# Exponent matmuls over all 128 rows in place of pairs in 64 rows, with a re-made issue list

## The chip, the cores and the metric

The kernel runs on one core of one Trainium2 chip. The metric is the device time of one execution in microseconds (us); the median of three runs is given, with the lowest and highest.

## The reference

Two independent branches work on 2048 positions and 576 channels each, and their outputs stand side by side. Branch A is a diagonal state-space model used as a long convolution: a kernel K is made for every channel from 128 complex exponentials, and u is convolved with it. Branch B is linear attention of 32 heads of 18 with a learned feature map.

```python
# A
A = -exp(log_A_real) + 1j * A_imag
C = (C_real + 1j * C_imag) * dt[:, None]
P = exp((A * dt[:, None])[:, :, None] * pos)          # 576 x 128 x 2048
K = 2 * einsum("dn,dnl->dl", C, P).real
y = irfft(rfft(u_t, 2 * L) * rfft(K, 2 * L))[:, :, :L] + u * D_skip
# B
q, k, v = split(x @ wqkv)
phi = lambda t: concat([softmax(t @ w_phi), softmax(-(t @ w_phi))])
kv, z = einsum("bhsf,bhsd->bhfd", phi(k), v), phi(k).sum(s)
out = (einsum("bhqf,bhfd->bhqd", phi(q), kv) / (phi(q) . z + 1e-6)) @ wo
```

## The kernel before

The kernel first records some 2459 operations, each with the engine that may do it, what it reads and writes, and a cost that a planner used. It then issues them in the order of a long written list, `ORDER`. A word of the list is the number of an operation; an `x` takes its second engine (ACT or DVE, DVE or POOL), `@` names the PSUM banks that it gets, and `:n` puts n filler matmuls ahead of it, which multiply zeros (line 237). So the order on every engine, the banks and the choice of engine all come from this list. All transfers are issued from SyncE's queue, SP, in list order.

Branch B runs through 16 key tiles (projections as `x` times `wh`, `wl`, `vh`, `vl`, each number split in two parts, 14 matmuls of 288 columns per half), a small turn of the sums (`kv`), and 16 query tiles (projection, softmax, transposes of `e` into `fT`, products with `kvb`, output projection). Branch A has u transformed in 16 steps (`ub` times `w1`), 36 groups of 16 channels that make K, its transform (`kfirst`), 16 frequency products (`ub`, `ff`), and 16 closing steps (`last`, `zi` times `w1`). Both branches are interleaved by the list.

A group makes its part of K from cosines and sines (`cs`, by POOL and ACT) and from magnitudes exp(m t). The exponents m t come from TensorE: `mg` holds log magnitudes in four parts of 16 channels, that is 64 rows, and holds the same 64 rows a second time in rows 64 to 127; `sel` is a constant with the times. `sizes_of` (its matmuls have line 295 in the profile, as all of `mm` do) makes the exponents for two groups at once: six matmuls of 512 columns into six PSUM banks, `M`, `up` and `dn` for each group. They are three operations of two matmuls each; one works in rows 0 to 63 and the other in rows 64 to 127 of the array. Over the two halves `sel` holds different columns (at, dn, up above, up, at, dn below), so that a pair reads the same 512 columns of `sel` and yields two different results. There are 18 such calls, 54 pairs, 108 matmuls. ACT then takes exp in PSUM (line 811), DVE multiplies them into the waves (lines 815 to 820), and 64 small matmuls (`g4`) sum over the 128 states.

The tensor engine works in differently split arrays: the projections use all 128 rows and columns, the pairs and the u steps two halves of 64 rows, `g4` and the key sums four strips of 32 columns, the frequency products 64 x 32 and 32 x 64. `mode` in the recorded operation names this split for the planner.

A tile name such as `ub`, `ff`, `zi` or `ot` is a pool of 5, 2, 2 and 3 buffers in turn; a load into one waits for whoever read the buffer last.

Of the kernel before, what the change touches and what calls it, by code (L numbers as in the profile page):

```python
# [276 lines left out]
def body(tc, nc, i, out, ctx):  # L277
# [16 lines left out]
    def mm(o, l, r, start=True, stop=True, skip=False):  # L294
        pe.matmul(o, l, r, start=start, stop=stop, skip_group_check=skip)  # L295
# [492 lines left out]
    def sizes_of(g, par):  # L788
        pl.at("group", g // 2)
        pl.step("g0")  # L790
        mg, gi = par[1], g % (NG // NB)
        b = [B("ps", [128, W, 32]) for _ in range(6)]

        def both(k):
            def f():
                for r, rs in enumerate((lo, hi)):
                    mm(b[2 * k + r].t.rearrange("p x y -> p (x y)"), mg.t[rs, gi + (2 * k + r) // 3, :], sel.t[rs, 512 * k:512 * k + 512])
            op("pe", 233, f, r=[mg, sel], w=b[2 * k:2 * k + 2], mode=(64, 128))
        for k in range(3):
            both(k)  # L800
        return b[:3], b[3:]
# [191 lines left out]
0 1 2 3 1097 1093 4 68 1094 5 1096 1154 1104 1105 1107 1092 1108 1109 51 34 1095 6 27 7@0:49 20 1106 1110 1111 1112 1113 1114 1115 8 35@2 1199 1137 11  # L993
28@4 29 52 12 1116 1120 9 53x 30 36 10 54 13 22@6 32 37 21 1117 39 992 1118 1119 40 15@0 14 1074 23 31 33 1121 38 1063 1003 344 18 25 16 345 24
1004@42:11 19 26 17 41 1073 287 1127 1077 56@6 47 42 288 1078 48 1122 1124 346x 1123 57 347x 1125 43 1126 44 45 60 1396 1076 1084 1006 1128 1129 289x
1130 1080 61 49 1075 348@0 1400 46 1131 349 1079 290 1138 291@6 1132 1161 1133 1134 352 62 1081 292 295 353 296 1082 354 1085 351@2 1083 350 355x 1397
1048 294@0 59@6 1086 1399 1135 55 1136 63 268 269 1155 361 1005 64 58 356 69 71 270x 297 360 1162 1156 1157 1398 271x 65 1158 171 1087 1064@24 1066 72
1200 1163 293 273@6 272 357 66 67 73x 1159 1164 1160 1065 1088 298x 1089 50@4 299 358 1090 1168 74 1165 70 304 359 1166 1167 77@2 300 276 1139 1401
301 277 1402 362 172 173x 1169 1170 1192 302 76 274@0 1140 275 80 278 1141 1403 1091 1148 1147 279 1149 1150 174 303 1193 1201 1151@56 1172 111 1098
1171 81 82 1152@72 305 285x 1099 79@0 1180 1174 112 1173 1175 78 1177 1176 1153@35 89 1178@6 1067 1068 1194 1183 284 1202 1203 1181 1184 83 1204 1195  # L1000
113 114 84 1196 1018 1007 75 1038 1205 1230 1197 1198 211 1182 1179 280 1185 1186 281 1231 282 179@0 177@2 1142 176 116@6 117 325 115 175 1206 85 180
181 182 1207 1208 183x 86 1143 283x 286 1190@52 1232 1233 1234 120 121 87x 1187@3 1218 1189@67 1235 1237 1238 1239 326 122 1221 1188 178 327 1209 1404
212 189 1211 328x 123x 88 118@2 330@0 90 119 213x 124 1210 1212 1214 1213 1191@67 184 129 1215 185 1220 188 1240 1144 1241 1216@5 214 1242 216@2 215
1145 1146 1269 91 1243 128 1236 1223 186 306 1268 187x 1224 1219 1222 92 1217 93 1405 1270 1271 331@6 219 220 94 332 1100 329 221 222 125 190 126 1419
1245 1406 333 1225@5 342x 1276 1275 1272 1277 1227@23 1244 1278 1246 1228@67 1247 334 127x 1249 1256 1226x 1248 191 335 223 218@0 1250 1252 1251 1253
217 1279 192 1280 193 130 1254@5 1273 307 228 1274 1259 336 194 1307 1049@20 1306 224 225 1051 1050x 341 1308 96@6 1282 1229@01 1258 337 1281 1257 97
1407 1262 338 197@2 339 100 101 196 1261 1260 199@6 308x 1052 1283 1284 198 226x 195 1412 227 1408 1409 1410 1411 1413 1255 200 1414 229 201 340x 1101
1263@5 230 202 1440 1415 1265@10 1102 209 1069@62 102 343 1314 1070x 95 1058 203 1285 1071 1266@23 1288 1287 1290 1286 98@6 1291 99 309 1313 1309 1315
1294 1264 1267@15 1289 231 204 103 1297 1072 1295 205 109 1292@0 1293 1316 1317 1318 232 1298 1310 1311 233 1312 311@2 1417 104 1320 1296 1319 1321x
105 1039@60 1300 206 208 1041 1040 106 310 313@0 312 207x 1299 314 315 1416 1418 1420 1421 1422 1423 1424 1425 1491 1059@62 108 1322 316 1426 1427  # L1010
1428 1492 1103 1061 210 323x 317 1060 1301@5 1304@23 1042 1303@67 1323 1484 322 1493 993 1033 235@0 131 249 234 1325 1324 1485 1486 1326 1327 132 1328
237@6 1302 1329 238 239 250 251x 1330@5 1487 107x 1447 110 1488 1331x 252 1062 1305@25 1349 1351 1350 240 1332 236 1352 1446 1448 1353 1355 247 318
# [82 lines left out]
```

## Time and profile before

| | |
|---|---|
| median of three runs | 544.55 us (543.78 to 545.48) |
| profiled execution | 545.11 us |
| its span, first to last instruction | 543.3 us |
| PE busy | 521.5 us (96%), 8192 matmuls |
| DVE, ACT, POOL busy | 455.9, 382.1, 328.8 us |
| bytes moved by DMA | 107.01 MB, 197 GB/s on average |
| granted TensorE clock | 0.998 |

A row of a group has line, engine, operation, names (written <- read), shape, count, then busy time and mean length of one, then idle time of the engine just before and what ended it. Matmul records overlap, so the step between matmuls is read from their starts in the timeline. PEld is TensorE's weight load, SPq the issuing of transfers.

### The profile page before, as it was taken

Reading aid. Unit: us, or ns where it says so; the run is one execution under the profiler, and the core shown is the slowest. Engines: PE = TensorE matmul, PEld = TensorE weight load, DVE = VectorE, ACT = ScalarE, POOL = GpSimd, SP = SyncE. Lnnn points to the kernel's source line nnn. Section 1 sums busy time; section 2 is a strip of 40 time slices with the busy share of each in tenths; the row PEclk is TensorE's granted clock in tenths of the full one; section 3 lists DMA queues with packets and bytes.
Section 4 is the critical chain, followed back from the end, with each engine's and each line's share of the span. In section 5 each row is a group of like instructions: output and inputs, shape, how many; then the busy total and the mean of one; then the engine's idle time right before and its main releaser. Section 6 shows DMA issues by size and latency. Waiting matters only on the chain.

```text
span 543.3 us, 19242 instructions
## 1 busy us (share of the span) xinstructions
PE 521.5 (96%) x8192; PEld 435.9 (80%) x8192; DVE 455.9 (84%) x716; ACT 382.1 (70%) x555; POOL 328.8 (61%) x456
## 2 busy tenths in 40 slices
PE   8999999999999989999999999999899999999995
PEld 7999899888888767888878666766689877776984
DVE  7999899898868889999989996999974889787641
ACT  4868798798559799889689977989733444343332
POOL 1173885958777775982758998997433617434300
PEclk9999999999999999999999999999999999999999
DMA  8936711244245678246664588756458789998785
GB/s 235 326 105 195 281 45 31 101 139 134 89 139 190 207 241 294 83 128 196 229 205 118 153 265 250 241 180 194 131 173 271 234 281 293 287 281 260 265 252 157
DMA packets 86163, 107.01 MB, mean 197 GB/s; under 512 B 5698, under 2 KB 70338, under 8 KB 86078
## 3 DMA queue, kind: packets, MB, share of 16 engines
q1 hardware_dynamic: 86078, 105.79, 61.5%
q8 instruction: 64, 1.05, 0.8%
q14 instruction: 21, 0.17, 0.1%
HBM read 61.22 MB, written 44.54 MB: 195 GB/s over the span
## 4 chain that ended last, share of the span: by engine, by line
PE 69%; DVE 13%; DMA 7%; ACT 4%; issue 3%; SPq 2%; POOL 1%; DVEq 0%; ACTq 0%; POOLq 0%
PE psum L295 63%; PE psum L549 3%; DMA ff<-in_ff_dram 2%; DMA dram<-zi 2%; PE psum L237 2%; DVE ac L314 1%; DVE cs L816 1%; SPq L979 1%; PE psum L577 1%; DMA cs<-dram 1%; DVE e L310 1%; DMA ub<-dram 1%; DVE e L314 1%; DVE small L434 1%; DVE small L437 1%
## 5 line engine op out<-in xcount | busy, mean ns | idle before, releaser
L295 PE MATMUL psum<-vh,x 128*128 128x288 f32 x576 | 123.6, 301 | 0.5 <-ACT ks L300 0.5
L295 PE MATMUL psum<-wh,x 128*128 128x288 f32 x576 | 124.1, 302 | 0.0
L757 POOL TENSOR_TENSOR cs<-cs,pi 128x32 int32<-128x32 int32 (+4 forms) x180 | 108.5, 608 | 8.0
L295 PEld LDWEIGHTS psum<-wh,x 128*128 128x128 f32 x576 | 94.1, 188 | 7.7 <-issue 4.2
L295 PEld LDWEIGHTS psum<-vh,x 128*128 128x128 f32 x576 | 94.0, 188 | 5.4 <-issue 3.2
L295 PE MATMUL psum<-vl,x 128*128 128x288 f32 x320 | 93.8, 295 | 0.0
L295 PE MATMUL psum<-wl,x 128*128 128x288 f32 x320 | 93.7, 295 | 0.0
L811 ACT ACTIVATE psum<-psum 128x512 f32<-128x512 f32 x108 | 59.9, 588 | 15.4 <-PE psum L295 14.9
L295 PEld LDWEIGHTS psum<-vl,x 128*128 128x128 f32 x320 | 60.2, 188 | 0.0
L295 PEld LDWEIGHTS psum<-wl,x 128*128 128x128 f32 x320 | 60.2, 188 | 0.0
L310 POOL TENSOR_TENSOR x<-zo,x 64x128 fp32r<-64x128 f32 (+1 forms) x30 | 25.4, 848 | 46.3 <-ACT x L394 35.1
L310 POOL TENSOR_TENSOR e<-e,small 128x1152 f32<-128x1152 f32 (+1 forms) x24 | 41.2, 1720 | 14.5 <-DVE small L450 7.8
L815 DVE TENSOR_TENSOR cs<-psum,cs 128x1024 f32<-128x1024 f32 x36 | 43.6, 1212 | 3.7 <-ACT psum L811 3.6
L310 POOL TENSOR_TENSOR e<-small,e 128x576 f32<-128x576 f32 x26 | 30.6, 1177 | 25.4 <-DVE small L437 23.6
L816 DVE TENSOR_TENSOR cs<-psum,cs 128x1024 f32<-128x1024 f32 x36 | 43.6, 1214 | 1.4 <-PE psum L295 1.3
L295 PE MATMUL psum<-ub,ff 64*32 64x288 f32 x1024 | 40.0, 410 | 4.3 <-DMA ff<-in_ff_dram 1.9
L295 PEld LDWEIGHTS psum<-kvb,fT 126*128 126x128 f32 (+1 forms) x320 | 38.3, 188 | 7.2 <-issue 2.9
L295 PEld LDWEIGHTS psum<-cs 128*32 128x32 f32 x2304 | 34.1, 110 | 11.2 <-issue 2.9
L295 PE MATMUL psum<-cs 128*32 128x64 f32 x2304 | 40.0, 220 | 2.6 <-DVE cs L816 0.9
L295 PE MATMUL psum<-kvb,fT 126*128 126x133 f32 (+1 forms) x320 | 41.6, 280 | 0.1
L440 ACT ACTIVATE e<-e 128x1152 f32<-128x1152 f32 x32 | 37.0, 1164 | 2.7 <-POOL e L310 1.3
L781 ACT ACTIVATE cs<-cs 128x1040 f32<-128x1040 int32 x36 | 38.3, 1064 | 0.6 <-POOL cs L776 0.4
(156 smaller groups left out, 1115.2 us busy)
## 6 DMA issues: line engine op xcount, KB each, us to landing
dram<-zi SPq DMA_DIRECT2D x32, 576.0 KB
ub<-dram SPq DMA_DIRECT2D x64, 288.0 KB
dram<-zo SPq DMA_DIRECT2D x32, 288.0 KB
zo<-in_xT_dram SPq DMA_DIRECT2D x24, 320.0 KB
zi<-dram SPq DMA_DIRECT2D x12, 576.0 KB
ub<-in_u_dram SPq DMA_DIRECT2D x16, 288.0 KB
xd<-x SPq DMA_DIRECT2D x8, 576.0 KB
x<-xd SPq DMA_DIRECT2D x8, 576.0 KB
```

The costliest lines, as they stand in the source:

```text
L237: self.matmul(t[0:cols, 0:n], self.zero.t[0:rows, 0:cols], self.data.t[0:rows].bitcast(BF16)[:, 0:n], start=not o[13], stop=not o[13], ski ...
L295: pe.matmul(o, l, r, start=start, stop=stop, skip_group_check=skip)
L310: op(eng, [c_dve(n[0]) if e == "dve" else c_pool(n[1]) for e in eng], lambda e: (dve if e == "dve" else pool).tensor_tensor(dst(), a(), b( ...
L314: op(eng, c_dve(n) if eng == "dve" else c_pool(n), lambda: e.tensor_tensor(dst(), a(), b(), op=alu), r=r, w=w, with_=with_, lock=eng == "p ...
L434: op("dve", c_dve(D), lambda: dve.tensor_reduce(two(top.t), v(), axis=AX.X, op=ALU.max, negate=True), r=[p], w=[top])
L440: op("act", c_act(1152) + 40, lambda: act.activation(e.t, e.t, AF.Exp), r=[e], w=[e], table="exp")
L549: pe.transpose(tp.t[0:m, j - j0, :], e.t[:, sign, 7 * g:7 * g + GRP[g], :].rearrange("p h f -> p (h f)"), ident.t)
L757: op("pool", c_pool(2 * n * W), lambda n=n, j=j: pool.tensor_tensor(x()[:, :, :, n:2 * n], x()[:, :, :, 0:n], pi.t[:, j:j + 2, gs].bitcast ...
L781: act.activation(cs.t[:, 1], cs.t[:, 1].bitcast(I32), AF.Sin, scale=TURN)
L811: op("act", c_act(512), lambda b=b: act.activation(b.t, b.t, AF.Exp), r=[b], w=[b], table="exp")
L815: op("dve", c_dve(64 * W), lambda: dve.tensor_tensor(F(), both(M.t), F(), op=ALU.mult), r=[M, cs], w=[cs])
L816: op("dve", c_dve(64 * W), lambda: dve.tensor_tensor(E.t[:, :, :, 32:64], both(up.t), cs.t[:, :, :, 0:32], op=ALU.mult), r=[up, cs], w=[E])
```

## The change

The constant `sel` is laid out as at, up, dn in its upper 64 rows and zero in its lower 64. Each of the six matmuls reads all 128 rows of `mg` and of `sel`; the second copy in `mg` meets zeros. The two matmuls of an operation are no longer in two halves of the array but one after the other, in the split that the projections use. The planner's cost of the operation goes from 233 to 470 ns. The list was made anew, by the change's author under the assumption of late transfers; it changes the order on all engines, banks, second engines (139 operations with `x` become 146), and fillers (118 become 160; 49 stand ahead of the first weight fold in both).

```diff
     at, up, dn = (np.repeat(x, W, 0) for x in (sel[:, 64:], sel[:, 32:64], sel[:, :32]))
-    sel = np.concatenate([np.concatenate([at, dn, up], 1), np.concatenate([up, at, dn], 1)])
+    sel = np.concatenate([at, up, dn], 1)
     r = np.arange(128)[:, None]
-    sel = np.concatenate([sel, r % W == np.arange(W), r // DH == np.arange(7)], 1)
+    sel = np.concatenate([np.concatenate([sel, 0 * sel]), r % W == np.arange(W), r // DH == np.arange(7)], 1)
...
         def both(k):
             def f():
-                for r, rs in enumerate((lo, hi)):
-                    mm(b[2 * k + r].t.rearrange("p x y -> p (x y)"), mg.t[rs, gi + (2 * k + r) // 3, :], sel.t[rs, 512 * k:512 * k + 512])
-            op("pe", 233, f, r=[mg, sel], w=b[2 * k:2 * k + 2], mode=(64, 128))
+                for r in range(2):
+                    h, s = divmod(2 * k + r, 3)
+                    mm(b[2 * k + r].t.rearrange("p x y -> p (x y)"), mg.t[:, gi + h, :], sel.t[:, 512 * s:512 * s + 512])
+            op("pe", 470, f, r=[mg, sel], w=b[2 * k:2 * k + 2])
...
 ORDER = """
-0 1 2 3 1097 1093 4 68 1094 5 1096 1154 1104 1105 1107 1092 1108 1109 51 34 1095 6 27 7@0:49 20 1106 1110 1111 1112 1113 1114 1115 8 35@2 1199 1137 11
```

Two places of the list. The first is PE at the time of 188 to 195 us of the profile before, where the pairs of two groups stand between steps of u (`ub,w`), a fold of the query weights (`fT,e`) and the sum of a group (`cs`). Before:

```order
L295 MATMUL psum<-ub,w_225 128x288 x4
L295 MATMUL psum<-sel,mg 128x512 x2
L295 MATMUL psum<-ub,w_225 128x288 x4
L295 MATMUL psum<-sel,mg 128x512 x2
L295 MATMUL psum<-fT,e 128x126 x5
L295 MATMUL psum<-sel,mg 128x512 x2
L295 MATMUL psum<-cs 32x64 x32
```

The three pairs take turns with two u steps and half a fold, without fillers. Now, from the second pair on:

```order
L237 LDWEIGHTS zero
L237 MATMUL psum<-ident,zero 128x256
L295 MATMUL psum<-sel,mg 128x512 x2
L295 MATMUL psum<-fT,e 128x126 x9
L295 MATMUL psum<-sel,mg 128x512 x2
L295 MATMUL psum<-cs 32x64 x32
L295 MATMUL psum<-fT,e 128x126 x2
```

Two fillers (the second is shown) stand ahead of the second pair, two more ahead of the first, and more of the fold has moved in front of the third pair.

The second place is SP's queue at the loads of frequency product 12, whose `ff` is used near 479 us of the profile before; the numbers of the buffers are kept. `dram_910` and `dram_5046` (now `dram_1156` and `dram_5117`) are the transforms of u and K. Before:

```order
L904 DMA ub_7270<-dram_5046 128x2x288
L904 DMA ub_7273<-dram_910 128x2x288
L895 DMA ff_7296<-in_ff_dram 128x512
L904 DMA ub_7319<-dram_5046 128x2x288
L904 DMA ub_7321<-dram_910 128x2x288
L979 DMA out_0_dram<-ot_7015 64x1x288
```

The `ff` load stands between the loads of `ub`, two of which follow it. Now:

```order
L905 DMA ub_7306<-dram_1156 128x2x288
L905 DMA ub_7308<-dram_1156 128x2x288
L905 DMA ub_7310<-dram_5117 128x2x288
L896 DMA ff_7316<-in_ff_dram 128x512
L967 DMA zi_7333<-dram_4805 128x1152
L957 DMA dram_6835<-zo_7314 128x2x288
```

Three `ub` loads stand together ahead of the `ff` load, and a load of `zi` and a store follow it.

More of the change, by code (lines that the diff above doesn't have):

```diff
@@ L997 @@
[L997 to L1000, printed above, removed]
@@ L1073 @@
[L1073 to L1075 removed]
+1104 1105 0 1107 1 4 2 6 1093 1108 1096 5 1106 7@6:49 27 34 1109 1110 1092 8 29@2 9 1111 51 1112 28 1097 11 1095 32 20 10 52 36@0 12 33 992 30 35 1113
+22@4 37 21 39 13 40 31 14@6 1114 1003 1115 25 38 23 53 15 1004@20:9 1116 18 26 1117 54 1120 1118 344 1075 1094 16 1076 345 1119 24 41 1121 1161 346x
@@ new lines @@
+17 1122 19 287 57@4 47 347 1080 348@6 1079 42 1127 1137 56 1123 1081 349 288 1124 1074 44 55 48 1125 1126 43 1005 1128 1129 45 1006 289x 60 290 1130
+291@2 49 1063 1138 1077 46 1082 1131 292 1132 1073 352 1396 1078 353 1133 1134 1084 350@0 268 1083 351 295 1154 1135 68 1136 71 58@6 61 3 1162 1139
+1086 360 269 1199 1085 270x 1163 62 361 1064@40 271 171 1164 63 59 354 1155 1066 296 64 1400 273@2 1087 1065 65 297 294@0 1399 1088 72 1165 998 66 293
+272 298x 1089 73x 50@4 1397 1090 1156 355 67 172 276 1091 69 1166 1200 70 1157 356 1158 74 1193 1147 1167 304x 1159 357 303 1160 299 358 77@6 1169
@@ new lines @@
+1201 76 277 300 359x 301 274@0 1149 80 362 1148 1168 1151@52 302x 1202 75 275 1170 81 305 111 278 1171 82 173 1152@63 279 285x 1180 1140 1192 1173 174
+1194 88 79@0 1174 1153@75 83 1177 1176 78 1172 280 1175 1182 1195 1183 1398 112 1178@6 1196 1203 1181 1401 325 1204 113x 177@2 1186 281 284 1237 114
+1197 89 1184 326 1238 1205 1198 91 1185 117@0 1239 176 1141 327 282 283x 180 181 84 328 116 1207 1206 179@2 286 1187@7 1142 182 1208 183 188 1231 175
+1179x 85 120 86 121 1190@56 122 115 87x 1218 184 1188x 1240 1230 1232 1189@01 1233 1221 178 1209 1212 123 1234 1210 1241 119@6 1067 1211 211 212 118
@@ new lines @@
+1215 1235 90 1214 213 92 1213 1236 1216@5 129 1143 1191@01 189 1048 185 1402 1220 1219 332@6 214x 216@2 1222 1144 215 1145 124 1403 1242 1243 1223
+1224 1245x 331 93 125 219 1146 1244 1099 1269 220 1217 94x 221 186 1227@30 330@1 329 187x 1404 190 222 1405 1246 1268 1270 191 993 126 1038 333 1225@5
+1276 1271 1248 1419 342 1228@67 334 1247 1249 127x 218@1 1250 335 217 1100 192 336 1150 1253 1275 223 128 337 1251 1277 130 1252 1226x 1272 193x
+1254@3 1307 1412 224 1098 306 1306 1278 225 95 228 1255 1256 1049@05 1406 194 1068 1308 1273 1407 96@2 1408 1259 226 1279 1051 97 307 100 101 227 338
@@ new lines @@
+1409 1050 1229@67 1258 1257 1410 1274 198@0 341 1309 102 197@2 1440 1282 1280 339 196 1261 1262 1260 195 200 1281 199 229 340x 249 308 1411 201 1263@7
+1283 1069@52 1284 209 1314 1265@01 309 250 1413 202 1414 343 1052 1264x 1285 1313 1070x 1266@56 1071x 203 1310 1286 1288 99@2 1289 1311 103 1415 1287
+1058 1267@07 98 1416 1290 104 1291 1295 1294 1297 1292@1 363 1315 204 230 311@5 109 1298 231 105 1296 1316 1293 251 1312 1317 1039@02 205 1318 1008
+1101 208 106 1007 310 1041x 1320 1417 1418 1040 1420 1300 312@0 313 1018 1319 1421 1072 206 1422 314 1321x 108 315 1299 207x 252x 232x 1322 1059@25
@@ new lines @@
+210 1423 1424 1060 1061x 323x 1301@7 1303@23 1304@56 1323 233 1102 131 151 234@0 1425 1326 1324 1426 1325 1328 1427 322 1327 1428 1349 1352 1329 235
+1485 1062 1439 1484 237@2 1330@6 107x 1302x 1486 1103 316 152 317 1033 110 1491 1305@57 238 1331 236 1492 1332 239 1351 1350 1447 1446 318 247 1354
+254@0 1353 1042 240 319 1487 153 1355 1448 1333@25 320 253 1493 1335x 1334x 132 133 1494 257 258 1495 1336 256@5 241x 1337@20 1496 1356@7 1488 321x
+1338 1339 259 260 1489 1454 1497 324 154x 1341@20 246 364 261 255 1342 1449 134 1453 262 242 265 243 155 263 266 1340 244 136@2 1343 1344 1490 1345@05
@@ new lines @@
+1346x 1499 137 245x 264x 1498 1450 1347x 157@0 140 141 1455 1019@25 1451 379 1020x 156 1357x 267 1481@32 1456 142 160 143 1500 248 1021 1457 458 1348
+161 1501 162 148 1482@56 1504 1452 1502 163 1510 1503 139@0 168 1505 1506 1507 1022 138 164 165 380 1458 149 1513 166 1508@5 1459 144 1460x 999@20
+1530 145 1001 381@6 1509x 1483@01 1000 1529 167x 1461x 382 1512 146 147x 1511 159@2 1515 1516 383 158 384 1514 169x 1517@5 385 1002 170 1531 150 386
+366 1522 394 1523 1524 1462 1518x 1034@20 1443@45:2 1036x 401 1009@06 1525 1463 1035x 1464 1444@23:2 1532 1011 1466 1013 135 403@6 1533 402 1010 387
@@ new lines @@
+1534 1465 1526 1467 1469 1527 395@0 1472 406 1535 1537x 404 1468 1528 1445@45 1470@2 1474 1471 396 1361 405 408 1473 399 1362 407 389@6 1536x 1475
+388:2 397 410@2 1363 392 1012 1477 1364 390 1028 1476 1365 409:1 413 1478 411 1479@5 1429 371@4 1366 1369 400 393 1480x 398 1368 367@5:2 391 424 412
+1538 415 1430 414 372x 994@60 365 1370 373 460@2 416 1367 1431 459:1 1371 995x 370 369 1372 368x 426@6 996 425 1373 1374 461 462 463 1432 1376 1037
+1688 1375x 417 374x 1433 1377 1043 1434 1044@40:1 1519@23:2 375 526 1435 427 428 1436 1539 1045x 1046 997 429 1437 1542 464 1520@67:1 1541 1545 1438
@@ new lines @@
+1544 465 1540 1548 430 1543 466 1014@40:6 1521@62:5 431 432 467 1546@3:2 1551 1016 433 1689 527@0 468 1691 1547 1015 1653 434 469 435 436 1550 1654
+376 1690 1655 1656 528 1549 437@4 470 1554 439@5 1553 377 441@7 1552 438 1358@32 1657 440 418 442 1378 1555@4 529 1658 530 1359@51 1660 531 1379 1692
+1661 378 532 446@7 1380 443@0 533 1662 1381 1663 1382 447 1556 471@2 1387 1664 1360@43 1659 448 1384 472 492 1383 444 1667 1441 1390 493@6 1385@2
+473@5 534 1389 419 1388 1665 1666 445 535 1386 475@1 1668 1393 449@02 1391 1392 494 420 536 1693 1017 474 421 450 451 1578 1694 495 476 1577 480@4
@@ new lines @@
+1669 1695 537 1394@3 1584 477@5 481 1579 1047 1395x 496 1585 1586 1557 482 1587 478 1558@06 479 483@54 1560 452 1559x 1580 538 594 543@3 1023 1053
+1562@06 453 1581 541@2 484 422 1582 485 1563 1588 539@5 497 1696 544x 1442 540x 1583 454@0 486 1564 1561 542 487 1589 1697 1570@46 1572x 1591 1590
+545@2 1592 546 1650@67 548@3 423 1571x 549 1698 1593 550 547 488@4 1699 1711 1670 489 1671 498 1700 1651@32 499 455 1701 1702 1573 1703 1673 1672 490
+1704 1674 1679 1675 1676 1705 1566@64 1677@3 456 500 1568 560 1682 1732 1652@01 501 1616 1706 1567 502 1565 1707 1680 503 1709 1681 1683 595@6 1615
@@ new lines @@
+551@54 552 1684 1678 596 1685 553 1054@20 1708 1686@5 554 1569 1710 597 504 2158 1712 1713 1055 555 598 1617 1056 1574@23:1 1622 1714 1024@06 1687
+1623 509@4:2 599 1715 1624 1594 1595 1057 1026 1025 1618 1619 1716 510 505@5 1731 1027 600 1597 1575@67 1625 1620 507@2:1 1596 506x 508 1029@40 511@2
+1603 1031 1599 1030x 1717 1598 1626 1600 1606 1576@45 1621 1718 601 1032 512 1627 562@0 628 1628 1604 2159 1605 1601@7 1721 1602x 1607 1608 1719 1720
+1609 514@6 1629 561:1 2153 1745 1746 1610@7:1 1630 1631 2152 513 2151 491 602 515 1747 1722 556@4:2 2154@2 1723 516 1724 1738 1748 1739 563 1611 1740
@@ new lines @@
+2054 1749 1750 603 564 1741 2156@0 1725 565 2162@6 2155 2160@2 566 2157 567 2163 2161 1726 517@01 557 518 604 1751 2047 1612@67 1632 519 1742 1727 605
+1635 2048 630@2 2046 1743 558 1613@04 520 521 1633 1753 1634 1636 1638 1637 1614@15 629 1643 1744 1641 1639@0 631 1752x 1642 606 568 523@6 2165 1754
+1784 559 1644 1645 1783 522 2164 1646 632 569 1785 2111 607@1 524x 1735@23 1647 1640 2051@6:1 633 2053 1648@0 1755 1786 2052x 1787 608 1788 1649
+2166@64 1758 1736@01 1756 609@2:2 2167 1759 2168 457 1757 1733 1760 1764 1761 1789 611@3 1776 1777 1778 570 610 612 2049@4 1773@62 1779 1728 1780
@@ new lines @@
+1737@73 1781 2050 1794 1765 1782 1766 1762@0 1791x 1831 1767 1769 1790x 1770 2057@4 1763 2055@0:1 1768 1793 616@3:1 2056 2109 2117 571 1792 525 2169
+1832 572 2110 613@7:2 1734 2058 1999 614 2059 2112@0:4 2114@4 2115 2170 615 2171 617 618 1771@7 573@4 1796 2116 1774@35 2113 2060 1839 1772x 634 1795
+1797 1838 2061@06 2062 1729 574 1799 575@2:1 1798 1819 619@67:2 1800@3 576 2131 620 1833 1840 2063 1801 2120@0 1822 1730 2064 621 1841 1834 577@4 578
+2121 2118@2 1775@65 622 635 2119 1802 1945 579@4 1820 1807@20 1998 1997 1821 623 1824 1842 662 1835 582@7 2065 1946 1808 580 1843 1825 1947 2123 581
@@ new lines @@
+1844 1815@24 1809 583 1846 584 1836 1823 2122 1817 585@01 586 1816x 587 2004 2000@6 2001 2124@24 2066 2005 588 2002@6 589 2125 2008@0:2 636 2003
+2006@4 2126 2009 1810 1818 2130 2132 1837 2010 2007 1845x 2011 2012 1948 625@6 2014x 2128 624 2138 1803@02 1847 626x 1811@64 1804 2013x 1805x 637 1812
+1813 2015@20 2127 1826@7 2016 1827 2135@4 2133@6 2136 1953 2134 2129 2096 2017 1952 2137 2141@4 1954 2018x 2022x 2021x 2020 2019x 2139@6 2142 1828@01
+1955 1956 590@2 1829@45 1949 2088 1950 1848 2089 1957 1958 2140 1849 1857 2143 1851 2090 1850 1951 1852 1830@67 591 1853 1854 1960 1959x 592x 1860
@@ new lines @@
+1926 1927 1902@3 687@67 1940@5 1903 1930 1929 1814 660 2038 1928 772 2040@03 688 773 689 808 1941x 809 1931@2 810 2041 690 691 1932 1980 1993@24:1
+2201 2042 1994x 593 1995 1981@06 708 1983 2044 1982x 1989@24 1996 709 1991 2043x 1990x 775@6 774 692@0 1985@24 1984 710 1987 776 777 733 778 779x
+812@6 2045 1986x 711x 734 1992 716@5 735 736 712@2 1988 844 811 813 814 714@4 780 781 693 715 713 717 721@2 815 718@3 782 694x 816 722 738@4 2368 845
+817 2179 846 723 2369@0 719 818 2370 720 2175@6 2180 783 2181@2 2183@0 2176x 737 695 784 881 724@67 2182 739 847 2389 725 2184 726 785 2187 882 883
@@ new lines @@
+727 2373 849@2 740 2244 786@0 2202 2200 2185 2375 728 848 884x 788@6 730@4 790@1 787 741 2186 850 2207 742 729 789x 851 819 2203@6 661 2189 791x 2188
+2390@2 731x 743 820 2205@4 2208 2391 2372 2204x 2211@0 2206x 732 2209@6 2190@24 2249 821 2191 2212 2210 2192 2193x 792@1:2 2196x 822 2243 795@0:1 744
+2394 2242 2197 2250 2214x 823@6 2194 793 2376@2 796 824 2195 794 797 2213x 2245@6:1 2377 2247@4 2246 852 2253@0 2251@2 2347 2199 2248 2198 2215@64
+2254 885@0 2334 2252 2256 2216 745 2217 798@45 2328 886 2326 853x 2327 799 800 825@2 887 2333 827@3 2218 2382 2219 888 801 2371 2255 2331@6 826 802
@@ new lines @@
+2332 2393 828 2329@0 2392 2335@4 2330 889 2337@2 2336 2257@60 832@4 2285 2220 2258 2286 803@0 2380 2395 890 2374 2338 829@5 2339x 2259 2260 2284 804
+833 2289@6 746 2291 2340x 830 2287@2 805 2288 2292 2383@0 891 2261 2262 892 834 2379 831 2290x 2341@46 2342 2306 747 835@32 836 2312 748x 2384x 2343
+854 2344 2295@0:2 2293@6:1 837 753@4 749@5:2 2307 838 751@3 2305 2296 839 841@0 855 2294 750 754 893 894 856 752 2345 2313 806 2378 2271 2310@2 895
+918 2308@6 2309 2297 2316@4 2314@6 2346 2311 2298x 896x 755@3 919 2317 758@2 2386 2315 756 920x 2299@46 2319x 840 921 759 757 2381 760 2264 2265 2270
@@ L1076 @@
+2404@2 2437 2416 2413 952 2415 2414 2405 986 987 2409 988@2 989 2426x 2407 2408 2406 953x 2430 990 2428 2429 2427 954 991
 """
```

94 lines of the change are left out of this document (16 added, 78 removed).

## The prediction

> **What bounds the kernel now.** I read the page first (busy shares, slices, chain), then the table by stage, then PE's groups by shape and PE's timeline around the exponent matmuls, and last who PE waits for.
>
> ```profile
> span 543.3 us, 19242 instructions
> ...
> PE 521.5 (96%) x8192; PEld 435.9 (80%) x8192; DVE 455.9 (84%) x716; ACT 382.1 (70%) x555; POOL 328.8 (61%) x456
> ...
> PE   8999999999999989999999999999899999999995
> ...
> PE 69%; DVE 13%; DMA 7%; ACT 4%; issue 3%; SPq 2%; POOL 1%; DVEq 0%; ACTq 0%; POOLq 0%
> ```
>
> PE is busy 521.5 of 543.3 us, full in nearly every slice, and holds 69% of the chain that ended last. So the program is PE's list of work plus the places where that list waits; an instruction added to PE costs its time unless it falls into such a place. The profiled execution took 545.11 us, its span 543.3, so 1.8 us lie around the span; it stands 0.56 us over the median 544.55. I make the sum as a difference and put it on the median.
>
> ```profile
> core 0: us, PE busy (x) PEld busy (x) DVE busy (x) ACT busy (x) POOL busy (x), PEclk, DMA share, GB/s
> ...
> 178.00:220.00 42.00, 37.17 (x609) 30.87 (x610) 36.21 (x62) 37.92 (x55) 29.45 (x45) 1.00 0.77 251
> 220.00:320.00 100.00, 98.14 (x1601) 80.17 (x1601) 96.46 (x164) 86.46 (x131) 74.36 (x116) 1.00 0.52 159
> ...
> 450.00:543.00 93.00, 85.33 (x1175) 68.70 (x1173) 58.08 (x102) 34.85 (x57) 31.62 (x25) 0.99 0.82 257
> ```
>
> The idle time of PE sits in two stretches: 178 to 220 (42.00 - 37.17 = 4.8 us), where ACT is the busiest engine, and after 450 (7.7 us, of them some 5.6 the tail), where DMA is (share 0.82). From 220 to 320 DVE is nearly as full as PE. The granted clock is full, so no part of the change can win by it.
>
> **Part 1: two 64-row matmuls become two 128-row matmuls (54 times).**
>
> ```profile
> L295 PE MATMUL psum<-wh,x 128*128 128x288 f32 x576 | 124.1, 302 | 0.0
> ...
> L295 PE MATMUL psum<-sel,mg 64*128 64x512 f32 x108 | 27.4, 487 | 2.6 <-ACT zi L300 1.2 <-DVE e L314 0.8 <-ACT zo L608 0.2
> ```
>
> The 487 ns are the length of a record, not PE's step, since records overlap; the step is read from starts. Here is a pair alone amid the projection matmuls:
>
> ```profile
> 103.85 0.30 PE L295 MATMUL psum<-wl,x 128*128 128x288 f32 x1
> 103.98 0.43 PE L295 MATMUL psum<-wh,x 128*128 128x288 f32 x2
> 104.25 0.29 PE L295 MATMUL psum<-wl,x 128*128 128x288 f32 x1
> 104.47 0.49 PE L295 MATMUL psum<-sel,mg 64*128 64x512 f32 x2
> 104.90 0.41 PE L295 MATMUL psum<-wh,x 128*128 128x288 f32 x1
> 105.14 0.29 PE L295 MATMUL psum<-wl,x 128*128 128x288 f32 x1
> 105.27 0.42 PE L295 MATMUL psum<-wh,x 128*128 128x288 f32 x2
> ```
>
> A 128-row matmul of 288 columns steps 0.13 us (103.85 to 103.98, 105.14 to 105.27). From the wl at 104.25 to the wl at 105.14 pass 0.89 us, where two steps without the pair would be 0.27: this pair cost 0.62. The pair itself is less; two pairs in a row show it:
>
> ```profile
> 95.07 0.73 PE L295 MATMUL psum<-sel,mg 64*128 64x512 f32 x4
> 95.75 0.40 PE L295 MATMUL psum<-vh,x 128*128 128x288 f32 x1
> ```
>
> 0.68 for two pairs, 0.34 each. So in the first view 0.62 - 0.34 = 0.28 went into the change of row split to 64 and back: a late start before (104.25 to 104.47 in place of 0.13: 0.09), a late start behind, and a first 128-row matmul that steps 0.24 in place of 0.13. That is 0.14 per change of split, bounded by the 0.09 of the entry alone and by 0.20 (0.09 drained plus the 0.11 of that slow first step).
>
> No row shows 512 columns over 128 rows. Bounds: 288 columns in 0.133 make 0.237 for 512; the filler matmuls, 256 columns, give the other end:
>
> ```profile
> 213.79 1.03 PE L237 MATMUL psum<-ident,zero 64*128 64x256 bf16 x8 [0.16 <-DVE zi L300]
> ...
> L237 PE MATMUL psum<-ident,zero 64*128 64x256 bf16 x34 | 4.5, 269 | 0.3 <-DVE zi L300 0.2
> ```
>
> Eight in 1.03 us, the last of them 0.27 long: (1.03 - 0.27) / 7 = 0.109 a step, 0.217 for 512 columns. Far above both lies 0.34, if that is what 512 columns of this type take in any split. I take 0.2275, the middle of the two near rows, because the 288-column matmuls are of the same type and the same 128 rows. Two of them make 0.455 where a pair took 0.34: 54 x 0.115 = **+6.2 us** (+5.1 to +7.2; +18.4 by the far end).
>
> The pairs no longer change the split where they stand among 128-row work. Counted along PE's list, the row or column split changes 240 times before and 205 times now: 35 x 0.14 = **-4.9 us** (-3.2 to -7.0). A single pair in a 128-row stretch thus falls from 0.62 to 0.455, while a second pair in a row rises from 0.34 to 0.455; the old list has 11 such double runs among 43, the new one 6 among 48. The change of `sel` itself is one DVE multiplication of the same size, and no DMA changes: nothing.
>
> Here the Trainium skill speaks against the change. "TensorE: Matmul & The Clock Gate", Part 3 on packing small matmuls, says that matmuls in different row tiles run at once, the second costing about 4 ns more, so each undone pair costs a whole further matmul; with its isolated step of N/2.4 + 2.5 ns a pair would be 0.22 and two matmuls 0.43 us, an estimate of +11.4 us, or 551 us with the splits above. The trace agrees that both start together, but not on the sum: the next pair starts after 0.34, so the rule's price for the pair is not met here, and the measured one decides.
>
> **Part 2: more fillers.** The zero matmuls that the list inserts go from 118 to 160; 49 stand at the start in both, so 69 become 111. At 0.109 the 42 cost +4.6 us if PE never waits where they stand, and nothing if it always does. The old ones stood in 12 later places, in runs of up to 11; the new in 51, mostly of one or two. At the place that waits most they do stand in the wait:
>
> ```profile
> 187.51 1.24 PE L295 MATMUL psum<-ub,w 64*128 64x288 f32 x8
> 188.37 0.61 PE L295 MATMUL psum<-sel,mg 64*128 64x512 f32 x2
> 189.61 1.24 PE L295 MATMUL psum<-ub,w 64*128 64x288 f32 x8 [0.63 <-DVE zi L300]
> 192.03 0.49 PE L295 MATMUL psum<-sel,mg 64*128 64x512 f32 x2 [1.18 <-ACT zi L300]
> 192.57 1.38 PE L295 MATMUL psum<-fT,e 126*128 126x126 f32 x10
> ```
>
> PE waits 1.18 us for ACT to empty a bank before the second pair, and the new list has two fillers exactly there. If the waits of 178 to 220 are gone, this cover is gone too. I take a third, **+1.5 us**: most new places are outside the stretches that wait.
>
> **Part 3: the new list, under late transfers.** The waits of PE (not of its weight loads) that a transfer ended:
>
> ```profile
> PE psum L295 <- DMA ff<-in_ff_dram: 1.9, 3, 0.9
> PE psum L295 <- ACT zi L300: 1.7, 2, 1.2
> ...
> PE psum L295 <- DMA ub<-dram: 1.5, 2, 1.2
> ...
> PE psum L295 <- DMA cs<-dram: 0.4, 1, 0.4
> ```
>
> 1.9 + 1.5 + 0.4 = 3.8 us are the most that earlier loads can give directly. One of them:
>
> ```profile
> 474.50 0.34 SPq L895 DMA_DIRECT2D ff<-in_ff_dram  x1
> 474.90 0.94 SPq L904 DMA_DIRECT2D ub<-dram  x2
> ...
> 474.50 4.36 DMA ff<-in_ff_dram
> ...
> 478.99 1.40 PE L295 MATMUL psum<-ub,ff 64*32 64x288 f32 x34 [0.94 <-DMA ff<-in_ff_dram]
> ```
>
> The ff of product 12 is issued at 474.50, lands after 4.36 us, and PE has waited 0.94. On SP's queue the new list puts that load behind its three ub loads and ahead of the zi load and stores, and three PE operations further ahead of its use. But ff has two buffers, and the load still waits for the last matmul of the product before (chain: PE until 474.48), which both lists place a projection half, two groups of transposes and a closing matmul ahead of the use. So the transfer moves by fractions of a microsecond, and I take half of the 3.8: **-1.9 us**. What is late next there is the ub load behind, and then DVE's products. SP's queue is walked in order, so a load moved ahead of stores delays only stores, which PE meets as late `ot` buffers on ACT.
>
> The moves on ACT, DVE and POOL (465, 716 and 452 operations become 461, 718 and 454) I cost at nothing: their work hides behind PE. Where DVE is 96.46 of 100 us full, that cover is thin, and a worse order there is the risk of the last rival.
>
> Sum: 6.2 - 4.9 + 1.5 - 1.9 = **+0.9 us**, 545.4 us: within what a measurement can tell from no change, which I set at 0.3%, 542.9 to 546.2 us.
>
> **Rivals.**
> - *The new list closes the waits.* Half of the 4.8 us between 178 and 220, all 3.8 of the transfers, and fillers that stand only in waits: 6.2 - 4.9 - 2.4 - 3.8 = -4.9, 539.7 us. For it: fillers at the very waits of the trace, so the list was made knowing them. Against: it moves few things far, and the chain exponent matmul, ACT, DVE, next matmul stays as short as it was in the worst place (both lists leave no PE work between the last pair and its use in group pairs 6 and 8).
> - *Unpairing costs a full pass* (the page's rule as a mechanism). Both matmuls of a pair start together and take 0.34; if 512 columns take 0.34 alone too, two take 0.68: 54 x 0.34 - 4.9 = +13.5, with fillers and waits as in my sum 557.6 us. It decides, with over 1.6 us lost, once 512 columns step more than 0.234 us: 54 x (0.468 - 0.34) = 6.9, less 4.9 and 0.4. Against: 0.237 by the row of the same type.
> - *The fillers are work.* The transfers are not late, the waits they were put into do not come, all 42 cost: 6.2 - 4.9 + 4.6 = +5.9, 550.4 us. For it: 51 places, most where the trace shows no idle PE. Against: the place at 192 us.
>
> **Chances.** The forecast 0.42, its own range 543 to 548 (0.07 faster, 0.22 same, 0.13 slower); closed waits 0.32; fillers as work 0.17; a full pass 0.09. Faster 0.39, same 0.22, slower 0.39. The range, 539 to 551.5, leaves out the full pass (0.09), the deeper part of the closed waits (0.07) and of the fillers (0.03).
>
> **What the next profile would show.** The group `sel,mg` 128*128 with starts 0.22 to 0.24 apart and no slow first step behind it when 128-row work follows; 0.34 would make the full pass right. PE's busy time up by 1 to 4 us. Filler rows with idle time on either side (hidden) or tight between neighbours (work). The wait on ff and ub under 2 us in sum; PE idle between 178 and 220 near 4 us, or near 2 if the first rival holds. I am wrong in kind if PE's idle time moves by more than 4 us either way, since then the order and not the matmuls set the result.

## The result and the profile after

The changed kernel takes 551.12 us (median of 4 runs, 550.64 to 553.25); the kernel before took 544.16 beside it (4 runs, 542.90 to 545.48). The ratio is 1.0135, 95% interval 1.0098 to 1.0172: slower by some 7 us. The forecast was 545.4 us, no change. The profiled execution took 550.73 us. Here and below, four executions of 700 to 983 us (one each of E1, E4, E15 and the kernel before) are left out of all ratios, and E1's profile, which is one of them, is not read.

The page of the changed kernel, its span, busy engines and the chain that ended last:

```profile
span 548.9 us, 19311 instructions
...
PE 527.7 (96%) x8234; PEld 444.8 (81%) x8234; DVE 457.3 (83%) x718; ACT 376.5 (69%) x551; POOL 333.2 (61%) x458
...
DMA 3%; PE 3%; SPq 2%; DVE 1%; issue 0%; POOL 0%; ACT 0%; ACTq 0%
```

The chain breaks off after 9% of the span this time, so it tells only of the end. The span grew by 5.6 us, PE's busy time by 6.2, and PE's idle time went from 21.8 to 21.2 us. That looks as if work had been added and nothing else, and it is misleading, as the fillers show. Their busy time (line 237) after the first 20 us, first in the kernel before, then in the changed one:

```profile
20.00:560.00 540.00, 8.14 (x58) 1.00 0.59 188
```

```profile
20.00:560.00 540.00, 19.58 (x102) 1.00 0.58 188
```

There are 58 and 102 of them (the rest of the 118 and 160 stand before 20 us), and their busy time rose by 11.4 us. At the 0.109 of a tight row the 44 more would be 4.8 us. The rest is that many stand alone or in twos inside a wait, and a lone record is 0.27 us long. A wait filled with zeros counts as busy PE, so PE's idle time no longer measures its waits.

The table by stage of the changed kernel, and two more rows of the kernel before:

```profile
core 0: us, PE busy (x) PEld busy (x) DVE busy (x) ACT busy (x) POOL busy (x), PEclk, DMA share, GB/s
178.00:220.00 42.00, 39.96 (x633) 32.92 (x630) 34.98 (x62) 38.45 (x60) 34.13 (x46) 1.00 0.65 218
220.00:320.00 100.00, 99.10 (x1611) 82.13 (x1611) 93.21 (x155) 88.86 (x135) 76.10 (x120) 1.00 0.55 178
320.00:390.00 70.00, 65.71 (x1196) 48.06 (x1197) 64.33 (x92) 59.67 (x84) 49.66 (x64) 1.00 0.57 176
390.00:450.00 60.00, 57.05 (x864) 47.81 (x864) 47.89 (x76) 23.00 (x40) 22.40 (x21) 1.00 0.74 232
450.00:549.00 99.00, 89.72 (x1211) 72.60 (x1209) 64.49 (x106) 35.36 (x62) 27.26 (x20) 0.99 0.80 255
```

```profile
320.00:390.00 70.00, 66.48 (x1200) 47.35 (x1198) 63.30 (x90) 59.81 (x86) 57.07 (x71) 1.00 0.71 222
390.00:450.00 60.00, 59.28 (x881) 50.22 (x882) 45.37 (x73) 26.36 (x46) 23.34 (x20) 1.00 0.72 226
```

Between 178 and 220 us PE's idle time fell from 4.8 to 2.0 us. Between 390 and 450, where PE had been full (59.28 of 60), it now idles 2.95. The new list gains early and loses late.

The exponent matmuls in the groups by shape, and a call of two amid the projection:

```profile
L295 PE MATMUL psum<-sel,mg 128*128 128x512 f32 x108 | 36.6, 430 | 0.1
```

```profile
284.99 0.29 PE L295 MATMUL psum<-vl,x 128*128 128x288 f32 x1
285.13 0.63 PE L295 MATMUL psum<-sel,mg 128*128 128x512 f32 x2
285.59 0.30 PE L295 MATMUL psum<-wh,x 128*128 128x288 f32 x1
285.72 0.30 PE L295 MATMUL psum<-wl,x 128*128 128x288 f32 x1
```

Two matmuls take 0.46 us (285.13 to 285.59), start 0.14 behind the one before, and the next steps 0.13: no change of split on either side. Behind such a change the first of the two is slower, as at 80.92 us, behind the sum of a group:

```profile
80.92 0.73 PE L295 MATMUL psum<-sel,mg 128*128 128x512 f32 x2
81.49 0.29 PE L295 MATMUL psum<-vh,x 128*128 128x288 f32 x1
```

There the two take 0.57. The waits ahead of the exponent matmuls, 2.6 us before, are 0.1.

Who PE waits for now, its longest rows but the start's:

```profile
PE psum L549 <- DVE e L310: 1.3, 1, 1.3
PE psum L295 <- DVE small L566: 1.3, 1, 1.3
PE psum L295 <- DVE ot L300: 1.1, 2, 1.0
PE psum L237 <- DVE cs L819: 1.1, 1, 1.1
PE psum L295 <- ACT ot L300: 1.0, 1, 1.0
```

No row names a transfer: the 3.8 us on `ff`, `ub` and `cs` are gone. In their place PE waits for DVE and ACT, partly in front of a filler (L237). The first row is the place that the trace explains best. DVE's and PE's timelines there:

```profile
408.33 0.76 DVE L300 COPY zi<-psum 128x576 f32<-128x576 f32 x1 [3.42 <-DMA dram<-zi]
409.00 0.18 DVE L314 TENSOR_TENSOR small<-small 128x32 f32<-128x32 f32 x1
409.11 0.75 DVE L434 TENSOR_REDUCE small<-psum 128x32 f32<-128x576 f32 x1
...
412.81 1.59 DVE L310 TENSOR_TENSOR e<-e,small 128x576 f32<-128x576 f32 x1
```

```profile
412.85 0.27 PE L549 MATMUL psum<-ident,e 128*72 128x128 f32 x1
414.46 0.74 PE L549 MATMUL psum<-ident,e 128*72 128x128 f32 x5 [1.34 <-DVE e L310]
```

A copy of `kfirst` into a `zi` buffer waits 3.42 us until the store that last read the buffer has landed. Behind it in DVE's queue stands the softmax of a query tile, whose last product ends at 414.40; PE needs it for the tile's transposes and has waited 1.34. In the kernel before, the same copy waits for the same kind of store, but with the softmax ahead of it and its last product given to POOL:

```profile
406.67 0.76 DVE L314 TENSOR_TENSOR e<-psum,small 128x576 f32<-128x576 f32 x1
407.46 0.75 DVE L437 TENSOR_REDUCE small<-e 128x32 f32<-128x576 f32 x1
409.19 0.76 DVE L300 COPY zi<-psum 128x576 f32<-128x576 f32 x1 [0.97 <-DMA dram<-zi]
```

```profile
409.82 1.17 POOL L310 TENSOR_TENSOR e<-small,e 128x576 f32<-128x576 f32 x1
```

```profile
412.64 1.25 PE L549 MATMUL psum<-ident,e 128*126 128x128 f32 x10
```

There the ten transposes run without a wait. So the transfer did not stop being late; another engine now waits for it, with more behind it. That this place costs 1.3 us is read from the trace; it was not tried by itself. (The run of the new list with the old pairs, E2 below, has the same wait of 1.3 us there.)

### The profile page after: what moved, and what is told of

It reads as the page before. It is cut to its first block, busy times and chain, and to the rows that moved or that the text cites. A ratio compares the mean times of both kernels' runs of the same rounds, so it can differ in the third digit from the quotient of the medians.

```text
span 548.9 us, 19311 instructions
## 1 busy us (share of the span) xinstructions
PE 527.7 (96%) x8234; PEld 444.8 (81%) x8234; DVE 457.3 (83%) x718; ACT 376.5 (69%) x551; POOL 333.2 (61%) x458
## 5 line engine op out<-in xcount | busy, mean ns | idle before, releaser
L310 POOL TENSOR_TENSOR x<-zo,x 64x128 fp32r<-64x128 f32 (+1 forms) x33 | 30.0, 909 | 43.5 <-ACT x L394 37.6
L310 POOL TENSOR_TENSOR e<-e,small 128x1152 f32<-128x1152 f32 (+1 forms) x24 | 42.5, 1772 | 19.9 <-DVE small L450 11.0
L300 ACT ACTIVATE zi<-psum 128x576 f32<-128x576 f32 x41 | 25.7, 647 | 27.7 <-PE psum L295 22.6
L310 POOL TENSOR_TENSOR e<-small,e 128x576 f32<-128x576 f32 x27 | 32.0, 1187 | 17.8 <-DVE small L437 17.7
```

The costliest lines, as they stand in the source:

```text
L300: op(("act", "dve"), (c_act(n), c_dve(n)), lambda e: act.activation(dst(), src(), AF.Copy) if e == "act" else dve.tensor_copy(dst(), src() ...
L310: op(eng, [c_dve(n[0]) if e == "dve" else c_pool(n[1]) for e in eng], lambda e: (dve if e == "dve" else pool).tensor_tensor(dst(), a(), b( ...
```

## The experiments

The theory after this reading (H, where an expectation names it): the form of the matmuls costs about what its slots say; the list costs the rest, gaining in its head and losing in its tail. Its rivals: the matmuls cost a full pass; the added fillers are work; the loss sits in one separable part of the list (the engines chosen, SP's queue) or one stretch of it. Each ratio is to the kernel before on the same chip; 1% is 5.45 us. E1 to E15 are the numbers in the labels.

**E1 and E2: one half of the change each.** E1 has the old list and the new matmuls, E2 the new list and the old pairs.

```diff
 # E1: the kernel after
-ORDER = after.ORDER
+ORDER = before.ORDER
 # E2: the kernel before
-ORDER = before.ORDER
+ORDER = after.ORDER
```

> The old list with the new matmuls alone. Theory M (the matmuls cost: two 128-row steps of 0.234 us where a pair took 0.34, and only part of it won back by fewer changes of split, 240 to 209): 54 x 0.128 = +6.9 less some 2.5, so 547 to 550 us, PE busy up by 3 to 6. Theory L (the re-made list costs, the matmuls are neutral, as the prediction's +1.3 said): 543 to 546 us.

> The new list with the old pairs in 64 rows. Theory M: the 4 to 5 us of the matmuls come back, 545 to 548 us, and if the list closed waits (PE waits on no transfer any more in the changed kernel) it may even go under 544. Theory L: 549 to 552 us, as the changed kernel.

E1: 546.76 us, ratio 1.0033 (1.0011 to 1.0055), +1.8 us. E2: 550.63 us, 1.0099 (1.0072 to 1.0127), +5.4. Together 7.2, and the whole change measured 7.4 by its ratio: the two halves add up, and some three quarters are the list. E1 lies between its two ranges, E2 in that of theory L. One part of E2's 5.4 is not the changed kernel's: counted along the traces, the pairs change the split 249 times in the new list and 240 times in the old, an estimated 1.3 us at 0.14 each, while the changed kernel has 205 changes.

PE's longest waits in E2 behind 346 us are for DVE and ACT:

```profile
PE psum L549 <- DVE e L310: 1.3, 1, 1.3
PE psum L577 <- ACT ot L300: 1.3, 1, 1.3
PE psum L237 <- DVE ac L314: 1.0, 1, 1.0
PE psum L237 <- DVE cs L815: 0.9, 1, 0.9
```

Summed over all rows behind 346 us, PE waits 3.1 us for DVE and ACT and 2.3 for transfers in the kernel before, 8.9 and 0.8 in E2, and 8.7 and none in the changed kernel.

**E3 and E4: no fillers but the 49 at the start**, in the new kernel and in the old.

```diff
-for word in ORDER.split():
+for word in re.sub(r":(?!49)\d+", "", ORDER).split():
```

> The changed kernel without its 111 later fillers (the 49 at the start stay). If fillers are work on PE: up to 111 x 0.109 = 12 us less, 539 to 545. If they all stand in waits: 550 to 552, no change. The slots of the trace hold 7.8 us of fillers; a third of them as work would give 548.5.

> The kernel before without its 69 later fillers (the 49 at the start stay). If they stand in waits: 543.5 to 545, no change. If they are work: up to 69 x 0.109 = 7.5 us less, 537 to 541; their slots in the trace hold 5.9 us.

E3: 553.43 us, 1.0153 (1.0108 to 1.0198), against 1.0135 with its 111 fillers. E4: 548.92 us, 1.0068 (1.0042 to 1.0094). Both are above all that was expected. Taking fillers out wins nothing in the new kernel and costs the old one 3.7 us. Why is seen in the stage rows of E4 around a place where the list has fifteen of them, then in those of the kernel before:

```profile
210.00:215.00 5.00, 3.73 (x28) 2.98 (x26) 4.91 (x8) 4.28 (x5) 3.23 (x4) 1.00 0.97 310
215.00:220.00 5.00, 2.99 (x12) 1.48 (x12) 4.85 (x7) 4.46 (x7) 3.07 (x4) 0.94 1.02 311
220.00:225.00 5.00, 4.97 (x77) 4.80 (x78) 4.97 (x10) 3.85 (x8) 4.36 (x9) 0.50 0.45 162
```

```profile
215.00:220.00 5.00, 4.12 (x87) 3.32 (x86) 4.84 (x7) 5.00 (x9) 4.41 (x7) 1.00 0.96 292
220.00:225.00 5.00, 5.00 (x61) 4.58 (x63) 4.83 (x10) 3.27 (x8) 4.56 (x8) 1.00 0.15 58
```

The third column from the end, PEclk in the table by stage, is the granted clock. Without fillers PE is busy 2.99 of 5 us, and in the next 5 us it gets half its clock; with the fifteen fillers it is busy 4.12 of 5 and keeps it. Over the whole profiled span the clock is 0.998 before and 0.987 in E4 (whose profiled execution, 553.31 us, is among its longer ones). Over all executions its median is 0.990 in E4 and 0.996 in the kernel before beside it; as PE is busy nearly throughout, that is some 3 of the 3.7 us (an estimate: 0.6% of 545). E3 has two effects in one. Its median clock, 0.9925 against the changed kernel's 0.998, is worth some 3 us by the same estimate, and by the ratios it is only 1 us behind the changed kernel, so some 2 us of its 111 fillers may have been work. (Its profiled execution, 557.3 us, is its longest: PE stops there three times, 5.1 us together, for nothing that the profile shows, ahead of 165 us, where the changed kernel has no fillers either.)

**E5, E6 and E7: half a list each**, with pairs. `keep` holds the operations that the head has issued.

```diff
 # E5: c = 914, about 209 us; E6: c = 1628, about 348 us
-ORDER = before.ORDER
+ORDER = after.ORDER[:c] + [w for w in before.ORDER if number(w) not in keep]
 # E7: c = 1615, about 346 us
-ORDER = before.ORDER
+ORDER = before.ORDER[:c] + [w for w in after.ORDER if number(w) not in keep]
```

> Pairs in 64 rows, the new list up to its 914th word (near 209 us), then the old list's order of what is left. Theory H (the new list's head is better, its tail worse): the trace of the new list with pairs is 3 to 5 us ahead of the old one at this place, and the old tail keeps that: 540 to 542 us. Theory D (a lead at the head is lost because the waits behind are set by transfers and other engines, whatever the list): 544 to 545.5.

> Pairs, the new list up to its 1628th word (near 348 us), then the old order. Theory H: the lead at this place is 2.2 us, kept: 542 to 543.5 us. Theory D: 544 to 545.5. If the tail is bad for what the head leaves behind (buffers and loads in flight) and not by its own order: 547 to 550, as the whole new list.

> Pairs, the old list up to its 1615th word (near 346 us), then the new order. Theory H: the new tail loses the 5.3 us that the trace of the new list loses from here to the last matmul, and 1 us more behind it: 549 to 551.5 us. Theory D: 544 to 546.

E5: 543.31 us, 0.9965 (0.9945 to 0.9984): faster than both kernels, by less than H's 540 to 542. E7: 553.35 us, 1.0132 (1.0096 to 1.0167), beyond H's 549 to 551.5. E6 missed H and D: 550.39 us, 1.0073 (1.0049 to 1.0098) where a gain was expected. So either the new list loses ahead of 348 us too, or, as the third case of its expectation has it, the old tail goes badly with what the new head leaves behind; the end of this section comes back to it. E5's stage rows, its gain and its stretch behind 390 us:

```profile
178.00:220.00 42.00, 39.31 (x632) 33.31 (x629) 35.94 (x64) 38.49 (x60) 34.93 (x48) 1.00 0.70 235
...
390.00:450.00 60.00, 59.12 (x920) 49.08 (x916) 45.21 (x74) 25.61 (x45) 24.33 (x21) 1.00 0.76 235
```

It has most of the new list's gain between 178 and 220 us (PE idles 2.7, not 4.8) and keeps the old list's full PE behind 390.

**E8: how much of a pair's time is hidden?** The kernel before with every pair issued twice.

```diff
-                for r, rs in enumerate((lo, hi)):
+                for r, rs in 2 * tuple(enumerate((lo, hi))):
```

> The kernel before with each of the 54 pairs issued twice over (same result), which shows what TensorE work at this place costs. If PE's list is the bound there, 54 x 0.34 = +18 us, 563. If the waits around the pairs take it up (some 9 us of them in the slots of the pairs), +9, 554. Under 550 would mean that these matmuls were never on the path.

554.92 us, 1.0165 (1.0137 to 1.0193), +9.0 us by the ratio. The 54 more pairs are 18.4 us at 0.34 each, so half of it was taken up by waits, as expected. This also bounds the matmuls' form: 0.11 us more per pair, in such places, need not show in full.

**E9, E10 and E11: which part of the tail.** E9 and E10 are E7 with, behind 346 us, the old engine for each operation, or the old order on SP alone; E11 is E7 with the switch at 399 us.

```diff
 # E9, behind word 1615 of E7
+the second engine (x) of a word as in before.ORDER
 # E10, behind word 1615 of E7
+the transfers' words in the order of before.ORDER
 # E11
-c = 1615
+c = 1881
```

> Old list to 346 us, new order behind it as in the run that came to 553.35 us (old to 346, then new), but every operation behind 346 us stays on the engine that the old list gave it; the new list moves some 35 operations of the tail from ACT or POOL to DVE and back (62 differ). 64-row pairs. If the moves onto DVE (its busy time from 355 us on rose from 137.5 to 145.6 us) make the loss, 545 to 548 us; if the order does, 551.5 to 554.5.

> Old list to 346 us; behind it PE, ACT, DVE and POOL in the new order with the new choices of engine, and only SyncE's queue in the old order. 64-row pairs. If the order of the transfers makes the loss (553.35 us with the new queue), 545 to 548 us; if the order on the computing engines does, 551 to 556, since the old queue then also fits the new order worse.

> Old list to about 399 us, the new order behind it, 64-row pairs. With the switch at 346 us the kernel took 553.35 us, and its trace had lost about 4.5 us by 381 us and 7 by 470. If the loss is made between 346 and 399 us, 545 to 547 us; if the new order behind 399 us loses by itself, 549 to 553. By the trace about half each: 548.

E9: 564.07 us, 1.0359 (1.0328 to 1.0391). E10: 558.88 us, 1.0269 (1.0231 to 1.0306). Both are slower than E7 and than all that was expected of them. E10's longest waits of PE behind 346 us:

```profile
PE psum L295 <- DMA ff<-in_ff_dram: 4.1, 2, 3.4
PE psum L295 <- DMA cs<-dram: 3.8, 2, 2.8
```

7.9 us of waits for transfers stand there, where E7 has 1.4. The new order on the other engines needs its own queue and its own engines: putting one of them back doesn't mend the loss, and these runs can't say whether either is a cause of it. E11: 548.12 us, 1.0073 (1.0048 to 1.0097): if the switch itself costs nothing, some 45% of E7's loss is made between 346 and 399 us and the rest behind, about half each as expected.

**E12: the new matmuls in E5's list.**

```diff
 # the kernel after
-ORDER = after.ORDER
+ORDER = E5.ORDER
```

> The list of the run that came to 543.3 us (new to 209 us, then old), with the 128-row matmuls in place of the pairs. If the form of the matmuls costs its slots, as it did under the old list (+1.8) and the new one (+0.5), 543.5 to 545.5 us; if the pairs' places in the old tail were made for the short pair, and two matmuls push DVE's work there, 546 to 549.

543.68 us, 0.9976 (0.9957 to 0.9995), against E5's 0.9965: the form costs 0.6 us here, within what these intervals can tell from nothing.

**E13, E14 and E15: the new queue alone, and where the head's gain is lost.** E13 is the kernel before with only SP's order behind 346 us new; E14 and E15 are E5 with the switch at about 257 and 295 us.

```diff
 # E13, behind word 1615 of before.ORDER
+the transfers' words in the order of after.ORDER
 # E14 and E15
-c = 914
+c = 1160 (E14), 1361 (E15)
```

> The kernel before, 64-row pairs, with nothing changed on PE, ACT, DVE and POOL; only SyncE's queue behind 346 us takes the new list's order (159 of its 345 issues then stand elsewhere). If the new order of transfers helps where it is put, as the assumption of late transfers has it, 542 to 544 us; if transfers are late by fractions of a microsecond only and the rest of the order decides, 545 to 548; if a queue fits only the order that it was made with (the old queue under the new order cost 5.8 us more), 549 to 552.

> New list to about 257 us, old behind it, 64-row pairs; beside the switch at 209 us (543.3) and at 348 us (550.4). If the new list's middle loses what its head gains and it does so before 257 us, 546 to 549; if the loss lies behind 257 us, 542.5 to 544.5.

> New list to about 295 us, old behind it, 64-row pairs. If the middle loses evenly between 209 and 348 us, 546 to 548; if all of it is lost at the last switch itself (348 us), 542.5 to 544.5; if it is lost by 295 us, 549 to 551.

E13: 563.72 us, 1.0348 (1.0318 to 1.0378), worse than any of its expectations. PE's longest waits behind 346 us:

```profile
PE psum L295 <- DMA zi<-dram: 5.6, 4, 2.8
PE psum L295 <- DMA ub<-dram: 3.2, 3, 1.9
PE psum L295 <- DMA cs<-dram: 2.0, 1, 2.0
```

A queue walked in order is tied to the order that it was made with, in both directions. E14: 544.92 us, 0.9993 (0.9972 to 1.0014), between its two ranges. E15: 547.02 us, 1.0019 (0.9996 to 1.0043), as for an even loss. With the switch at 209, 257, 295 and 348 us the new list stands at -0.35, -0.07, +0.19 and +0.73%, and at +0.99% to its end (E2).

By these medians alone the loss would begin behind 209 us and be spread over the rest, but each of these kernels also pays for its switch, if that costs anything. The traces of the lists without a switch say something else. I took the matmuls without the fillers, each at its usual step (the median distance of starts where PE doesn't wait), and compared the times at which two kernels had done the same amount. E2 is ahead of the kernel before by 1.9 us at 209 us and by 1.4 at 346 (the expectations of E5 and E6 had 3 to 5 and 2.2), then behind by 1.5 at 399 and 4.3 at 535. The changed kernel is ahead by 0.5 and 0.8, then behind by 2.5 and 5.4. From 346 to 535 us the three traces with the new list there lose 6.2 (changed kernel), 5.7 (E2) and 7.7 us (E7), those with the old list there 0.4 (E5), 1.7 (E14), 1.4 (E15) and 0.6 (E6). So the new list loses behind 346 us, where the waits for DVE and ACT shown under E2 stand. What E6, E14 and E15 lose against E5 the traces don't show: each is one execution, and E6's is its fastest. E15's stops for 2.27 us at 198 us, in a group's sum, for nothing that the profile shows; E2's, with the same list there, does not.

## Why the prediction was wrong

**What bounds the kernel** was right: PE's list and its waits. The test that was set, PE's idle time, was not: it moved by 0.6 us while the list cost 5.4, because added fillers stand in waits and count as busy.

**Part 1 was right.** The step was taken as 0.2275 us and measured 0.23 (0.46 for two). Matmuls and splits were +6.2 - 4.9 = +1.3, and +1.9 under E1's old list, where the split changes 209 times and not 205; E1 measured +1.8 (+0.6 to +3.0). The full pass is out: it needed 0.34 for every step, and only the first matmul behind a change of split takes that long, which the sum counts with the change. "TensorE: Matmul & The Clock Gate" of the Trainium skill, Part 3, whose rule for packed matmuls would have made the two matmuls 11.4 us dearer (an estimate from its figures), does not agree: its price for the pair is what is not met, since a pair stepped 0.34, not about 0.22.

**Part 2 left out the clock.** I took a third of the added fillers as work, +1.5, and the last rival took all. That rival's 550.4 us is near the measured time, but not by its mechanism: without the 111 the kernel is not faster (E3), and without its 69 the kernel before is slower by 0.68% (E4). The +1.5 itself is neither borne out nor refuted, since no run takes out the 42 added ones alone and up to 2 us of E3's 111 may have been work. The prediction saw that "the granted clock is full, so no part of the change can win by it", and did not ask what keeps it full.

**Part 3 is the step that failed: the new list, taken as -1.9, or -0.4 with its fillers, measured +5.4 with them (E2).** Two parts of it came as the rival of closed waits had them: the waits for transfers went (3.8 us to none), and more than half of the idle time between 178 and 220 us. E5 shows what the second is worth with the old order behind it: -1.9 us, while 3.5 us of its waits for transfers stayed. The sentence that failed is the one that costs the moves on ACT, DVE and POOL at nothing because "their work hides behind PE". Behind 346 us it didn't hide: PE's waits for DVE and ACT went from 3.1 us to 8.7 in the changed kernel and 8.9 in E2. I had named the danger, and put it in the wrong place: that a load ahead of stores delays only stores, "which PE meets as late `ot` buffers on ACT". Such a wait came (at 533 us ACT waits 2.60 us for the store of an `ot` buffer, and PE 1.0 us behind it), but at the place traced PE met a late store on DVE, at a `zi` buffer with a softmax behind it (409 to 414 us), in a stretch that was full before. I weighed one place of SP's queue and one of PE's, and none of DVE's behind 390 us.

What stays open: which single moves of the list make these waits, since none was put back alone with its surroundings kept. E9, E10 and E13 show that the parts of a list can't be exchanged one at a time, so they can't tell whether the new order of the transfers would be good with another order of the work. It is also open why E14, E15 and E6 lose with the old list behind their switch: at the switch itself, or in the new list's middle in executions other than the profiled ones. That the list is worse because it was made for transfers later than they are is likely, and not shown.

## What to carry to other kernels

When a change comes with a re-made order, the order is a change of its own: cost it stage by stage, above all in the stretches that are full now, and ask for each in-order engine what stands behind the operation that waits for a transfer. Run the two halves apart, and then the head of one order with the tail of the other; here that gave a kernel (E5, ratio 0.9965) that beats both lists. Don't read filler matmuls as work that can be saved, nor PE's idle time as its waits where fillers stand; compare instead when two kernels have done the same amount of work.

## What was not expected of the hardware

The clock falls without one long gap. At the place shown of E4 the longest idle times of PE between 210 and 222 us are these:

```profile
215.01 0.51 PE L295 MATMUL psum<-sel,mg 64*128 64x512 f32 x2 [1.28 <-DVE e L314]
...
220.03 1.94 PE L295 MATMUL psum<-cs 128*32 128x64 f32 x64 [0.88 <-DVE cs L816]
```

No gap is longer than 1.28 us, yet the clock of the following 5 us was 0.50; the 64 matmuls of a group's sum then took 1.94 us in place of 1.10 in the kernel before. The Trainium skill, "TensorE: Matmul & The Clock Gate", Part 1 on oscillation, gives as the abstract rule that idle gaps should stay under about 3.4 us. Staying under it was not enough here: several gaps of at most 1.28 us, with PE busy 60% of 5 us, went ahead of the half clock. In the kernel before, which has some fifteen zero matmuls of 0.109 us at this place and gaps of at most 0.89 us, the clock stayed at 1.00.
